# One main body for all engines, without a block and its closing barrier, and output tile 14 issued by ACT

## Chip, core and metric

The kernel runs on one NeuronCore of a Trainium2 chip. The core has a matrix engine (TensorE, PE in the profile; its weight loads are shown as PEld), a vector engine (VectorE, DVE), a scalar engine (ScalarE, ACT), GpSimd (POOL) and SyncE (SP), which issues transfers and waits. Each engine runs its own instructions in its own order, and they meet through semaphores only. The metric is the device time of one execution in microseconds, lower is better.

## What is computed

Two branches on the same input `x` (2048 positions of 512 channels, bfloat16), mixed by a gate for each position:

```python
x = A_x
g = _sigmoid((x * gate_w).sum(-1, keepdims=True))
a = _A_ref(x, A_wqkv, A_wo)
b = _B_ref(x, B_w1, B_b1, B_w2, B_b2)
return g * a + (1 - g) * b
```

Branch A is a dilated sliding attention of 32 heads with 16 channels each: every position attends to itself and to the positions 2, 4, ... 14 before it, and the result is projected by `wo`. Branch B normalizes each position, mixes along the 2048 positions by `w1` (to 1792 hidden rows), applies gelu, and mixes back by `w2`.

## The kernel before

The program is not written engine by engine. It is a list of operations, each with its engine, an estimated duration, and the names that it reads and writes; a planner (`_Sched`, lines 72 to 283) orders them. `schedule` runs a list scheduler three times: at each step it takes, over all engines, the ready operation with the earliest start, ties going to the one with the longest work behind it (`bl`). A transfer counts as an operation of its issuing engine (`dma`, 0.5 us of issue for an output write). `plan_waits` then gives every operation the semaphore waits that it needs and that its engine doesn't know to be met already. The result is one list of operations for each engine.

`emit_engine` (lines 969 to 995) writes such a list out: for each operation its waits, then its instruction, then the increment of its semaphore. Behind SP's list it puts waits for all output writes, one semaphore for each of `ds_out[0]` to `ds_out[3]` and one for `ds_outb`:

```python
            if eng_name == OUTQ:
                for d in ds_out + [ds_outb]:
                    n_ = len([o for o in sch.ops if o.is_dma and o.dsem is d])
                    if n_:
                        e.wait_ge(d.handle, 16 * n_)
```

Line 336 opens a block, `nc.Block()`. Lines 997 to 1015 call `emit_engine` inside five functions, `block.sync` to `block.tensor`, so that each engine's instructions form a body of that engine; on leaving the block, all engines meet in a barrier: each drains its pipeline, GpSimd collects their arrivals and releases them. The profile puts these closing instructions at L335, the line of the `with` that holds the block, and the opening instructions (constants written by GpSimd, and a barrier that the program always begins with) at L1029.

The work goes in this order. Loads, the first of them transposing, bring `x` and the weights in (L430, L461 and L468 are the helpers that issue transfers). TensorE projects q, k and v (L594), with some warming matmuls before (L526), and VectorE forms the products of q and shifted k (L665), which TensorE sums over the heads' channels (L673). Then TensorE does the two large mixes of branch B, L787 with `w1` and L837 with `w2`, while VectorE does the softmax and the weighted sum of v, and ACT issues 32 copies (L430) that spread the attention weights. ACT adds the bias and scales branch B by 1 - g (L904).

The last stage is the projection by `wo`. `emit_wo` (lines 863 to 883) is called for the 16 output tiles of 128 positions each. For tiles 0 to 11 a tile is one piece of 512 columns, for tiles 12 to 15 two halves, a and b, of 256 columns: four matmuls (L853) and one eviction on VectorE (L874), which multiplies by g and adds branch B's value. Behind the evictions the tile is written to the output, tiles 0 to 14 by one transfer of 128 KB on SP's queue, with the semaphore `ds_out[i % 4]`, tile 15 by two of 64 KB: its first half on SP, its second on ACT with `ds_outb`.

Of the kernel before, what the change touches and what calls it, by code (L numbers as in the profile page):

```python
# [13 lines left out]
D = 512  # L14
# [4 lines left out]
NST = S // 128  # L19
# [269 lines left out]
def _views(nc, es):  # L289
    off = {}  # L290
    cur = [0]

    def region(name, nbytes):
        nbytes = (nbytes + 63) // 64 * 64
        off[name] = cur[0]
        cur[0] += nbytes

    region("X", NST * D * 2)
    region("XT", 4 * S * 2)
    region("WQKV", 4 * 3 * D * 2)  # L300
    region("W1W", 4 * NST * 256 * 2)
    region("PBUF", 2 * 4 * S * 2)
    region("WO", 4 * D * 2)
    region("Q5", 4 * S * 2)
    region("K5", 4 * KROW * 2)
    region("V5", 4 * KROW * 2)
    region("ATX", 8 * NW * HC * 2)
    region("ATT", NW * SC * 2)
    region("OUTS", 4 * D * 2)
    region("BR", 128)  # L310
    region("BT", 128)
    region("IDENT", 128 * 2)
    region("RP", 32 * 2)
    region("SMALL", 2048)
    total = cur[0]
    arena = es.enter_context(nc.sbuf_tensor("arena", [128, total], U8))

    def view(name, dtype, dims, extra=0):
        base = arena[:].bitcast(dtype)
        pstride = base.ap[0][0]  # L320
        esz = mybir.dt.size(dtype)
        assert off[name] % esz == 0
        return bass.AP(base.tensor, off[name] // esz + extra, [[pstride, 128]] + [list(d) for d in dims])

    def pview(name, dtype, p0, np_, dims, extra=0):
        base = arena[:].bitcast(dtype)
        pstride = base.ap[0][0]
        esz = mybir.dt.size(dtype)
        return bass.AP(base.tensor, p0 * pstride + off[name] // esz + extra, [[pstride, np_]] + [list(d) for d in dims])

    return view, pview, off, total


def bass_gated_mix__sliding_local_dilated__mixer_token_mlp__prompt_kernel(nc, A_x, A_wqkv, A_wo, B_x, B_w1, B_b1, B_w2, B_b2, gate_w, out, dbg=None):
    with contextlib.ExitStack() as es:  # L335
        block = es.enter_context(nc.Block())
        view, pview, off, total = _views(nc, es)
        ps = es.enter_context(nc.psum_tensor("ps", [128, 8, 512], FP32))
        esem = {e: es.enter_context(nc.semaphore("sem_" + e)) for e in ("pool", "act", "dve", "pe")}
        sch = _Sched()  # L340
# [6 lines left out]
        outv = out[0].rearrange("(t p) d -> p t d", p=128)  # L347
# [21 lines left out]
        T1 = view("X", BF16, [(D, NST), (1, D)])  # L369
# [33 lines left out]
        def col(v_, i):  # L403
            return bass.AP(v_.tensor, v_.offset + i, [list(v_.ap[0]), [1, 1]])
# [24 lines left out]
        def mk_dma(dst, src):  # L429
            return lambda e: e.dma_start(dst, src)  # L430
# [115 lines left out]
        for hf in range(2):  # L546
            t0 = 8 * hf
            for t in range(t0, t0 + 8):
                A("dve", (lambda t_: (lambda e: e.bn_stats(out=ST6[:, t_, :], in_=X[:, t_, :])))(t), 0.59,  # L549
                  reads=["x%d" % t], writes=["st6_%d" % t], name="ln1_%d" % t, prio=0)  # L550
# [13 lines left out]
              reads=["zc%d" % hf], writes=["sd%d" % hf], name="ln_sqrt%d" % hf, prio=0)  # L564
            A("dve", (lambda t0_: (lambda e: e.reciprocal(out=cols(RSTD, t0_, 8), in_=cols(SD, t0_, 8))))(t0), 0.25,
              reads=["sd%d" % hf], writes=["rstd%d" % hf], name="ln_rstd%d" % hf, prio=0)
# [43 lines left out]
        for (b0, d0, d1) in ((0, 0, 1), (0, 1, 2), (0, 2, 3), (0, 3, 4), (4, 0, 2), (4, 2, 4)):  # L610
            s0, s1 = 0, 512
            for b in range(b0, b0 + 4):
                tn, dl = first[b]
                last_main[0] = A("pe", f_proj(tn, dl, 0, b, d0, d1, s0, s1), 0.216 * (d1 - d0) * (s1 - s0) / 512,
                                 reads=["xt0h%d" % (d0 // 2)] + ["wqkv%d_%d" % (tn, dt) for dt in range(d0, d1)],
# [11 lines left out]
        for (tn, dl, sb) in seq_proj:  # L627
# [3 lines left out]
                             reads=xr + ["wqkv%d_%d" % (tn, dt) for dt in range(4)],  # L631
# [15 lines left out]
        for t in range(NST):  # L647
# [7 lines left out]
          reads=["th"], writes=["g"], name="g_g", prio=0)  # L655
        A("dve", lambda e: e.tensor_scalar(out=OMG, in0=TH, scalar1=-0.5, scalar2=0.5, op0=ALU.mult, op1=ALU.add), 0.15,
          reads=["th"], writes=["omg"], name="g_omg", prio=0)
        A("dve", lambda e: e.tensor_tensor(out=C2, in0=OMG, in1=B2C, op=ALU.mult), 0.15,
          reads=["omg", "b2c"], writes=["c2"], name="g_c2", prio=0)
# [25 lines left out]
        for wh in range(2):  # L685
# [6 lines left out]
            for (dl, c0, nc_) in pieces:  # L692
# [3 lines left out]
                  reads=["q5_%d_%d" % (dl, sb) for sb in range(c0, c0 + nc_)] +  # L696
# [3 lines left out]
            for wl in range(4):  # L700
                qop = A("pe", f_qkr(list(enumerate(bufs)), (wl,)), 0.92, reads=rd, writes=["lg%d_0" % (4 + wl), "lg%d_1" % (4 + wl)],
                        name="qkr_%d_%d" % (wh, wl), prio=-100 + wl, delay=BURST_DELAY)
                A("act", (lambda wh_, wl_: (lambda e: e.activation(out=ATT[:, :, 4 * wh_ + wl_, :], in_=ps[:, 4 + wl_, :].rearrange("p (h c) -> p h c", h=2), func=AF.Copy)))(wh, wl),  # L703
                  0.55, reads=["lg%d_0" % (4 + wl), "lg%d_1" % (4 + wl)], writes=["lw%d" % (4 * wh + wl)],
                  name="lev_%d_%d" % (wh, wl), prio=0)
# [24 lines left out]
        for hf in range(2):  # L730
# [3 lines left out]
              reads=["outs1"], writes=["lh%d" % hf] + (wall if hf == 0 else []), name="sm_sub%d" % hf, prio=0)  # L734
            if hf == 0:
                A("act", lambda e: e.activation(out=col(SD, 0), in_=col(ZC, 0), func=AF.Exp, scale=0.0), 1.5,
                  reads=["zc0"], writes=["sd0"], name="sm_pre")
            A("act", (lambda hf_, l_: (lambda e: e.activation(out=ATT[:, hf_], in_=l_, func=AF.Exp)))(hf, lgh), 1.95,  # L738
              reads=["lh%d" % hf], writes=["att%d" % hf], name="sm_exp%d" % hf, prio=0)
        for hf in range(2):  # L740
# [5 lines left out]
            def f_rcp(e, hf_=hf):  # L746
# [6 lines left out]
              reads=["rs%d" % hf], writes=["att%d" % hf], name="sm_nrm%d" % hf, prio=0)  # L753
# [4 lines left out]
        for u in range(8):  # L758
            c, hf = u // 2, u % 2
            ds_at = sch.dsem("atx%d" % u)  # L760
            for a_ in range(4):
                dst = bass.AP(ATX.tensor, ATX.offset + a_ * pst + u * NW * HC, [[4 * pst, 32], [1, NW * HC]])
                sch.dma("act", mk_dma(dst, psub(ATT, 32 * c, 32, hf * NW * HC, [(1, NW * HC)])), 32 * NW * HC * 2, ds_at, issue=0.62,
                        reads=["att%d" % hf], writes=["atx_%d_%d" % (u, a_)], deps=pb_readers, name="d_atx_%d_%d" % (u, a_))
        USEQ = [0, 2, 1, 3, 4, 6, 5, 7]
        for k_, u in enumerate(USEQ):
# [6 lines left out]
              reads=v_res + ["atx_%d_%d" % (u, a_) for a_ in range(4)], writes=[pn] + [qk_res, k_all][k_ % 2], name="avm_%d" % u)  # L773
# [30 lines left out]
        for ft in range(NFT):  # L804
# [5 lines left out]
              reads=["acc%d" % bank, "b1c"], writes=["ut%d" % ft] + ALLXT + ["xt0h0", "xt0h1"],  # L810
              name="gel_%d" % ft, prio=0)
# [30 lines left out]
        def WB(i):  # L842
            return (4 + i) % 8

        def WBN(i):
            b_ = WB(i)
            return ["acc%d" % b_] if b_ < 4 else ["lg%d_0" % b_, "lg%d_1" % b_]
# [10 lines left out]
        ds_out = [sch.dsem("out%d" % k) for k in range(4)]  # L858
        ds_outb = sch.dsem("outb")
# [3 lines left out]
        def emit_wo(i):  # L863
            parts = [(0, D)] if i < HT0 else [(0, D // 2), (D // 2, D)]
            ons = []
            for h, (c0, c1) in enumerate(parts):
                k_ = i if len(parts) == 1 else HT0 + 2 * (i - HT0) + h
                bank, bn = WB(k_), WBN(k_)
                sfx = "" if len(parts) == 1 else "ab"[h]
                frac = (c1 - c0) / D  # L870
                on = "o%d%s" % (i, sfx)
                ons.append(on)
                A("pe", f_wo(i, bank, c0, c1), 0.866 * frac, reads=["ot%d" % (i // 2), "wo"], writes=bn, name="wo_%d%s" % (i, sfx), prio=0)
                A("dve", (lambda i_, b_, c0_, c1_: (lambda e: e.scalar_tensor_tensor(  # L874
                    out=T1[:, i_, c0_:c1_], in0=ps[:, b_, 0:c1_ - c0_], scalar=col(G, i_), in1=T1[:, i_, c0_:c1_],
                    op0=ALU.mult, op1=ALU.add)))(i, bank, c0, c1), 0.08 + 0.67 * frac, reads=bn + ["g", "t1_%d" % i], writes=[on],
                  name="cmb_%d%s" % (i, sfx), prio=0)
                if i == NST - 1:
                    q = "act" if sfx == "b" else "sp"
                    sch.dma(q, mk_dma(outv[:, i, c0:c1], T1[:, i, c0:c1]), 128 * (c1 - c0) * 2,  # L880
                            ds_out[i % 4] if q == "sp" else ds_outb, issue=0.5, reads=[on], name="d_out%d%s" % (i, sfx))
            if i < NST - 1:
                sch.dma("sp", mk_dma(outv[:, i, :], T1[:, i, :]), 128 * D * 2, ds_out[i % 4], issue=0.5, reads=ons, name="d_out%d" % i)

        p3bank = {}

# [8 lines left out]
        for i in range(NST):  # L895
# [4 lines left out]
            elif i > 1:  # L900
# [5 lines left out]
              reads=["acc%d" % bank, "omg", "c2"], writes=["t1_%d" % i, "x%d" % i],  # L906
              name="t1_%d" % i, prio=0)
# [61 lines left out]
        def emit_engine(eng_name, e):  # L969
            for op in sch.order[eng_name]:  # L970
                for d in op.waits:
                    if d.is_dma:
                        e.wait_ge(d.dsem.handle, 16 * d.seq)
                    else:
                        e.wait_ge(esem[d.eng], d.seq)
                r = op.fn(e)
                if dbg is not None:
                    rr = r[-1] if isinstance(r, list) else r
                    dbg.setdefault("opmap", []).append((eng_name, op.name, rr.ins.name, op.start, op.end))
                if op.is_dma:  # L980
                    r.then_inc(op.dsem.handle, 16)
                elif op.sig:
                    if isinstance(r, list):
                        r = r[-1]
                    r.then_inc(esem[eng_name], 1)
            if eng_name == "sp" and dbg is not None and "keep" in dbg:
                for d in sch.dsems:
                    n_ = len([o for o in sch.ops if o.is_dma and o.dsem is d])
                    if n_ and d.queue == "sp":
# [4 lines that stand above are left out]
                    if n_:  # L994
                        e.wait_ge(d.handle, 16 * n_)

        @block.sync
        def _(e):
            emit_engine("sp", e)

        @block.gpsimd
        def _(e):
            emit_engine("pool", e)

        @block.scalar
        def _(e):
            emit_engine("act", e)

        @block.vector
        def _(e):  # L1010
            emit_engine("dve", e)

        @block.tensor
        def _(e):
            emit_engine("pe", e)


# [26 lines left out]
```

## Time and profile before

| | us |
|---|---|
| median of three runs | 169.53 |
| lowest and highest | 168.92, 169.91 |
| the profiled execution | 169.25 |
| its span, first to last instruction | 167.5 |
| outside the span (169.25 - 167.5) | 1.75 |
| TensorE matmuls busy | 163.4 |
| VectorE busy | 150.8 |
| ScalarE busy | 74.7 |
| granted TensorE clock, mean | 1.000 |

The span is what the rows of the profile cover; what lies outside it is not resolved by any row. In the rows, a `q` behind an engine's name means its sequencer: waits, branches, drains and issues of transfers, which don't count as busy time. `EVENT_SEMAPHORE` is a wait or a semaphore update of its own, `DRAIN` waits until the engine's pipeline is empty. In a timeline row come start, length (both us), engine, line, operation, written and read tensor, and the count of instructions merged into the row. In the row of a line come shortest, median and longest duration in ns, and the starts of the first and the last in us.

### The profile page before, as it was taken

The numbers are of one execution on the slowest core, as the hardware profiler recorded it, in microseconds if no ns is written. First come the engines' busy times: TensorE is split into PE (matmuls) and PEld (weight loads), VectorE is DVE, ScalarE is ACT, GpSimd is POOL, SyncE is SP. The second block draws the span as 40 slices with busy tenths as digits, with TensorE's granted clock in tenths as the row PEclk, the third lists the DMA queues.
The fourth block names the chain that finished last, engine by engine and source line by source line (L and its number), as shares of the span: only waits on it lengthen the run. The fifth ranks groups of instructions, "written<-read, shape, count | busy, mean of one in ns | idle before, by whom it ended". The sixth has DMA issues, their size and how long they took to land.

```text
span 167.5 us, 2155 instructions
## 1 busy us (share of the span) xinstructions
PE 163.4 (98%) x857; PEld 77.5 (46%) x857; DVE 150.8 (90%) x155; ACT 74.7 (45%) x115; POOL 0.8 (0%) x8
## 2 busy tenths in 40 slices
PE   8899999999999999999999999999999999999993
PEld 2355555544554444444444444444444444444462
DVE  0019999999999998799999999999999999999995
ACT  3087788888899827881221221231321312210000
POOL 1000000000000000000000000000000000000000
PEclk9999999999999999999999999999999999999999
DMA  5999999979204849996799806373574380000554
GB/s 129 256 253 225 239 342 301 291 230 294 83 0 122 287 137 250 297 257 162 167 295 330 270 10 157 92 210 84 145 219 126 94 223 0 0 0 0 185 181 139
DMA packets 47625, 29.64 MB, mean 177 GB/s; under 512 B 9856, under 2 KB 46464, under 8 KB 47616
## 3 DMA queue, kind: packets, MB, share of 16 engines
q1 hardware_dynamic: 45664, 24.98, 55.6%
q10 hardware_dynamic: 1952, 4.52, 9.8%
q8 instruction: 7, 0.11, 0.3%
q14 instruction: 2, 0.02, 0.0%
HBM read 21.11 MB, written 2.10 MB: 139 GB/s over the span
## 4 chain that ended last, share of the span: by engine, by line
PE 93%; DMA 3%; DVE 2%; issue 0%
PE ps L787 29%; PE ps L837 29%; PE ps L594 25%; PE ps L853 6%; PE ps L673 4%; DMA arena<-in_A_x_dram 3%; DVE arena L874 2%
## 5 line engine op out<-in xcount | busy, mean ns | idle before, releaser
L787 PE MATMUL ps<-arena 128*128 128x512 bf16 x224 | 48.7, 379 | 0.0
L837 PE MATMUL ps<-arena 128*128 128x512 bf16 x224 | 48.7, 379 | 0.0
L665 DVE TENSOR_TENSOR arena<-arena 128x4096 bf16<-128x4096 bf16 (+2 forms) x14 | 35.7, 2590 | 10.2 <-ACT arena L605 10.2
L594 PE MATMUL ps<-arena 128*128 128x512 bf16 x192 | 41.8, 380 | 0.7 <-DMA arena<-in_A_x_dram 0.7
L772 DVE TENSOR_TENSOR arena<-arena 128x8192 bf16<-128x8192 bf16 x8 | 35.0, 4418 | 0.0
L787 PEld LDWEIGHTS ps<-arena 128*128 128x128 bf16 x224 | 21.8, 98 | 26.6 <-issue 0.4
L837 PEld LDWEIGHTS ps<-arena 128*128 128x128 bf16 x224 | 21.9, 98 | 26.5
L594 PEld LDWEIGHTS ps<-arena 128*128 128x128 bf16 x192 | 21.6, 113 | 21.1 <-issue 1.8
L904 ACT ACTIVATE arena<-ps,arena 128x512 bf16<-128x512 f32 x16 | 12.4, 778 | 39.4 <-PE ps L837 39.4
L775 DVE TENSOR_TENSOR arena<-arena 128x4096 bf16<-128x4096 bf16 (+1 forms) x16 | 27.0, 1751 | 0.0
L605 ACT ACTIVATE arena<-ps 128x512 bf16<-128x512 f32 x32 | 18.6, 596 | 4.7 <-PE ps L594 4.7
L808 ACT ACTIVATE arena<-ps,arena 128x512 bf16<-128x512 f32 x14 | 9.6, 687 | 22.9 <-PE ps L787 17.3
L853 PE MATMUL ps<-arena 128*128 128x512 bf16 (+1 forms) x80 | 14.2, 337 | 0.0
L602 ACT ACTIVATE arena<-ps 128x512 bf16<-128x512 f32 x16 | 9.0, 596 | 7.5 <-PE ps L594 7.4
L573 ACT ACTIVATE arena<-arena 128x512 bf16<-128x512 bf16 x16 | 12.2, 808 | 0.0
L874 DVE SCALAR_TENSOR_TENSOR arena<-ps,arena 128x512 bf16<-128x512 f32 (+1 forms) x20 | 11.5, 638 | 0.6 <-PE ps L853 0.4
L853 PEld LDWEIGHTS ps<-arena 128*128 128x128 bf16 x80 | 7.8, 98 | 6.2
L649 DVE SCALAR_TENSOR_TENSOR arena<-arena 128x512 bf16<-128x512 bf16 x16 | 10.0, 684 | 0.0
L549 DVE BATCH_NORM_STATS2 arena<-arena 128x6 f32<-128x512 bf16 x16 | 9.9, 680 | 0.0
L719 DVE TENSOR_TENSOR arena<-arena 128x512 bf16<-128x512 bf16 (+4 forms) x11 | 7.3, 667 | 1.2 <-ACT arena L738 0.8
L673 PE MATMUL ps<-arena 128*32 128x512 bf16 x128 | 7.3, 380 | 0.0
L703 ACT ACTIVATE arena<-ps 128x512 bf16<-128x512 f32 x8 | 4.7, 592 | 3.7 <-PE ps L673 3.7
(38 smaller groups left out, 39.2 us busy)
## 6 DMA issues: line engine op xcount, KB each, us to landing
arena<-in_B_w_dram SPq DMA_DIRECT2D x7, 1024.0 KB, 8.2
arena<-in_B_w_dram SPq DMA_DIRECT2D x8, 896.0 KB, 5.2
arena<-arena ACTq DMA_DIRECT2D x32, 128.0 KB, 2.7
arena<-in_A_x_dram SPq DMA_DIRECT2D x4, 512.0 KB, 5.8
out_dram<-arena SPq DMA_DIRECT2D x15, 128.0 KB, 1.7
arena<-in_A_x_dram SPq DMA_DIRECT2D x1, 1536.0 KB, 7.9
arena<-in_A_wqkv_dram SPq DMA_DIRECT2D x2, 256.0 KB, 3.8
arena<-in_A_x_dram SPq DMA_DIRECT2D x2, 256.0 KB, 3.2
```

The costliest lines, as they stand in the source:

```text
L573: A("act", (lambda t_: (lambda e: e.activation(out=X[:, t_, :], in_=X[:, t_, :], func=AF.Identity, scale=col(RSTD, t_), bias=col(NMR, t_)) ...
L594: ins = e.matmul(ps[:, bank, s0:s1], lhsT=lhsT, rhs=XT[:, dt, sb * 512 + s0:sb * 512 + s1], start=(dt == 0 and s0 == 0), stop=(dt == 3))
L605: return lambda e: e.activation(out=dst, in_=ps[:, bank, :], func=AF.Copy)
L665: return lambda e: e.tensor_tensor(out=PBL[buf][:, :, 512 * c0:512 * (c0 + nc_)], in0=in0, in1=in1, op=ALU.mult)
L673: ins = e.matmul(ps[32 * c:32 * c + 32, 4 + wl, :], lhsT=RP, rhs=PBL[buf][:, wl, c * 512:(c + 1) * 512], start=(dl == 0), stop=(dl == 3), ...
L772: A("dve", (lambda o_, i0, i1: (lambda e: e.tensor_tensor(out=o_, in0=i0, in1=i1, op=ALU.mult)))(pv, in0, in1), 4.4, reads=v_res + ["atx_% ...
L775: A("dve", (lambda pv_, n__: (lambda e: e.tensor_tensor(out=pv_[:, 0:n__], in0=pv_[:, 0:n__], in1=pv_[:, n__:2 * n__], op=ALU.add)))(pv, n ...
L787: ins = e.matmul(ps[:, bank, :], lhsT=W1W[:, slot, st, 128 * e_:128 * e_ + 128], rhs=X[:, st, :], start=(st == 0), stop=(st == NST - 1))
L837: ins = e.matmul(ps[:, bank, :], lhsT=W2S[slot][:, ft, 128 * e_:128 * e_ + 128], rhs=UT[:, ft, :], start=(ft == 0), stop=(ft == NFT - 1))
L853: ins = e.matmul(ps[:, bank, 0:c1 - c0], lhsT=OT[:, t, 128 * i:128 * i + 128], rhs=WO[:, t, c0:c1], start=(t == 0), stop=(t == 3))
L874: A("dve", (lambda i_, b_, c0_, c1_: (lambda e: e.scalar_tensor_tensor(out=T1[:, i_, c0_:c1_], in0=ps[:, b_, 0:c1_ - c0_], scalar=col(G, i ...
L904: A("act", (lambda i_, bank_: (lambda e: e.activation(out=T1[:, i_, :], in_=ps[:, bank_, :], func=AF.Identity, scale=col(OMG, i_), bias=co ...
```

## The change

The block is not opened any more. The five engines' lists are written one after the other straight into the program's main body, by a loop over the engines; there are no bodies to branch into, no branch out of them, and no barrier behind them. The opening barrier at the program's beginning is not touched, and neither are SP's final waits for the output semaphores. Tile 14's output write is given to ACT's queue in place of SP's, and its semaphore is `ds_outb` in place of `ds_out[2]`; SP's final waits count accordingly.

```diff
-        block = es.enter_context(nc.Block())
         view, pview, off, total = _views(nc, es)
...
             if i < NST - 1:
-                sch.dma("sp", mk_dma(outv[:, i, :], T1[:, i, :]), 128 * D * 2, ds_out[i % 4], issue=0.5, reads=ons, name="d_out%d" % i)
+                q = "act" if i == NST - 2 else "sp"
+                sch.dma(q, mk_dma(outv[:, i, :], T1[:, i, :]), 128 * D * 2, ds_out[i % 4] if q == "sp" else ds_outb, issue=0.5, reads=ons, name="d_out%d" % i)
...
-        @block.sync
-        def _(e):
-            emit_engine("sp", e)
-
-        @block.gpsimd
-        def _(e):
-            emit_engine("pool", e)
-
-        @block.scalar
-        def _(e):
-            emit_engine("act", e)
-
-        @block.vector
-        def _(e):
-            emit_engine("dve", e)
-
-        @block.tensor
-        def _(e):
-            emit_engine("pe", e)
+        for eng_name, e in (("sp", nc.sync), ("pool", nc.gpsimd), ("act", nc.scalar), ("dve", nc.vector), ("pe", nc.tensor)):
+            emit_engine(eng_name, e)
```

## The prediction

> **What bounds the kernel now.** I read the head of the page first, then the chain of waits, and then the rows of the first and the last microsecond one by one, because the change touches only these two ends.
>
> ```profile
> span 167.5 us, 2155 instructions
> PE 163.4 (98%) x857; PEld 77.5 (46%) x857; DVE 150.8 (90%) x155; ACT 74.7 (45%) x115; POOL 0.8 (0%) x8
> q8 instruction: 7, 0.11, 0.3%
> ```
>
> ```profile
> 0.73 0.07 issue
> 0.80 4.44 DMA arena<-in_A_x_dram
> 5.25 0.14 issue
> 5.38 32.11 PE ps L594 x148
> ...
> 154.49 6.92 PE ps L853 x32
> 161.41 0.03 issue
> 161.44 3.98 DVE arena L874 x9
> ```
>
> TensorE is busy for 98% of the span, and from 5.38 to 161.41 us the chain is nothing but its matmuls. No edit touches a matmul, its operands or its waits, so some 156 us stay as they are. What can change lies before 5.38 and after 161.44. At the head the chain is the first transposing load from 0.80 to 5.25, started 0.07 us after the opening barrier let SP go. At the tail it is the last evictions of VectorE, up to 165.42, and then the following stretch, in which no compute engine works:
>
> ```profile
> 165.45:167.02 1.57, 0.00 (x0) 0.00 (x0) 0.00 (x0) 0.00 (x0) 0.00 (x0) 1.00 0.52 162
> 167.02:167.50 0.48, 0.00 (x0) 0.00 (x0) 0.00 (x0) 0.00 (x0) 0.00 (x0) 1.00 0.00 0
> ```
>
> The columns are the stretch, its length, busy time of PE, PEld, DVE, ACT and POOL with instruction counts, clock, DMA share and GB/s. The first stretch is the last output write in flight. In the second nothing moves at all: the granted clock is 1.00, the DMA engines stand still, and 0.48 us go by between the last landing and the end of the span. That is where the closing barrier is:
>
> ```profile
> L335 POOLq EVENT_SEMAPHORE  x2: 17/17/17, 167.3 to 167.4; - x2
> L335 POOLq DRAIN  x1: 557/557/557, 0.9 to 0.9; - x1
> L335 PEldq DRAIN  x1: 2155/2155/2155, 162.8 to 162.8; - x1
> L335 DVEq DRAIN  x1: 524/524/524, 164.9 to 164.9; - x1
> L335 ACTq DRAIN  x1: 152/152/152, 165.9 to 165.9; - x1
> L335 SPq COMPARE_BRANCH  x1: 33/33/33, 167.1 to 167.1; - x1
> L335 SPq DRAIN  x1: 7/7/7, 167.3 to 167.3; - x1
> L335 SPq EVENT_SEMAPHORE  x1: 17/17/17, 167.4 to 167.4; - x1
> ...
> L335 PEldq EVENT_SEMAPHORE  x1: 51/51/51, 167.4 to 167.4; - x1
> ```
>
> and SP's waits just before it:
>
> ```profile
> L995 SPq EVENT_SEMAPHORE  x2: 28/28/28, 166.6 to 167.0; - x2
> ```
>
> The columns are line, engine, operation, count, shortest/median/longest in ns, and first and last start in us. The reader is to see the order: SP's last wait on an output (L995) at 167.0, the branch out of its body at 167.1, its drain at 167.3, POOL collecting and releasing at 167.3 and 167.4, all engines let go at 167.4. Four of the five drains began long before the last landing, and only SP's is late. So the closing barrier costs what SP does after its last wait, and nothing else.
>
> **The change part by part.** The closing barrier goes. SP then ends with its waits on the output semaphores. There are five of them; in the old kernel two instructions at L995 and the branch share them, so the branch's share becomes one more wait of about 28 ns (L995's duration) in place of the branch's 33 ns, in the same place. What falls away is the time from the branch's end to the span's end: 167.5 - (167.1 + 0.03) = 0.37 us. The starts are printed to 0.1 us, so 0.27 to 0.47; the stretch of 0.48 us after the last landing is the ceiling, since SP must still see that landing. I take 0.37.
>
> The drains of the other engines fall away too. They cost nothing now: POOL's 557 ns begin at 0.9 us, PE's 2155 ns and DVE's 524 ns end at 165.0 and 165.4, ACT's 152 ns at 166.1, all under the last write, which is in flight until 167.02. Were a drain made up for behind the span, the dearest one that such an idle engine would need is POOL's 0.56 us.
>
> The opening. No branch into the bodies shows in the trace, so it is bounded: the engine that matters is SP, whose gap between the release and the first load is the 0.07 us "issue" at 0.73. A jump there can cost at most 0.07, and at least nothing, if the bodies followed the opening code directly. The opening barrier itself stays. PE's gap speaks for little: it is let go at 0.7 for 51 ns, and its first weight load starts at 0.81, in this row:
>
> ```profile
> L1029 PEldq EVENT_SEMAPHORE  x1: 51/51/51, 0.7 to 0.7; - x1
> ...
> 0.81 0.14 PEld L526 LDWEIGHTS ps<-const-bfloat16-1.0 128*128 128x128 bf16 x2 [0.81 <-issue]
> ```
>
> I take 0.03, about the middle. All of it would count, because the load at 0.80 is on the chain and TensorE is full behind it.
>
> By the Trainium skill (Runtime: NRT & Kernel Launch, Instruction fetch mechanics) a taken branch to a page that isn't at hand stalls its engine for a fetch by DMA. The q8 row gives the price of one fetch here: 0.3% of 16 engines' 167.5 us is 8.0 us over 7 packets, 1.15 us each. By that rule the opening and the closing branch would give back up to 2.3 us, 167.2 in place of 169.5. The stretch from 0.73 to 0.80 and the one from 167.1 to 167.3 are too short to hold such a fetch, so the trace speaks against the rule here, and it is only rival D.
>
> Output tile 14 on ACT. One issue of 128 KB leaves SP's queue and enters ACT's, with the semaphore of tile 15's second half. The rows are:
>
> ```profile
> 164.50 0.92 DVE L874 SCALAR_TENSOR_TENSOR arena<-ps,arena 128x256 bf16<-128x256 f32 x2
> 164.57 0.33 SPq L430 DMA_DIRECT2D out_dram<-arena  x1
> 164.93 0.48 DVE L874 SCALAR_TENSOR_TENSOR arena<-ps,arena 128x256 bf16<-128x256 f32 x1
> 165.01 0.37 SPq L430 DMA_DIRECT2D out_dram<-arena  x1
> 165.45 0.36 ACTq L430 DMA_DIRECT2D out_dram<-arena  x1
> ```
>
> ```profile
> L430 SPq DMA_DIRECT2D out_dram<-arena x16: 332/333/813, 154.2 to 165.0; - x16
> L430 ACTq DMA_DIRECT2D arena<-arena x32: 477/616/1194, 74.9 to 104.5; - x32
> DMA to landing us min/median/max: 1.6/1.7/2.4
> ```
>
> The evictions are those of tile 15's two halves (the first row merges both, the third is the second alone). SP's two issues are tile 14 and the first half of tile 15, ACT's is the second half. The lower fence has the issue times of all output writes and of ACT's copies, and the time to landing of all output writes. SP is through with tile 14 at 164.57 + 0.33 = 164.90. The eviction that tile 15's first half waits for ends at 164.50 + 0.48 = 164.98, and the issue follows at 165.01. So SP holds nothing up, and taking tile 14 from it brings nothing: gain 0. In ACT's queue tile 14 would be issued at about 164.57 too. With the 0.36 us of ACT's own output issue ACT is free at 164.93, with the median of its 128 KB copies, 0.62, at 165.19, and it is needed again when the last eviction ends at 164.93 + 0.48 = 165.41. Both are early enough: loss 0. The one issue as long as 1.19 would end at 165.76 and make tile 15's second half about 0.35 late; this end I keep for the range. Behind tile 14's issue in ACT's queue stands only that second half, and the final wait of SP waits for it. The two writes also share 16 DMA engines as before; tile 14's data is 0.88 us of issue ahead of the second half's, so its landing should stay at 1.6.
>
> In the planner (an estimate per engine of 0.5 us for either queue) nothing depends on an output write, so no other order should move.
>
> **The sum.** Against the profiled execution, 169.25 us with 1.75 us outside its span: 0.37 at the end, 0.03 at the opening, 0 for tile 14 make 0.40, so 168.85, and a span of 167.1. The median of the three runs shown is 169.53, 0.28 above the profiled one, and carried over to it the forecast is 169.13. I give 169.1.
>
> **The rivals.**
>
> A, the time outside the span shrinks too. The 1.75 us outside it are not resolved. If what follows the program is again a meeting of the engines, four of them now reach it early (POOL after 1.5 us of the span, the others by 165.8), where they came at once with SP before. The nearest row for what that could hide is the longest drain of an idle engine, 0.56; with 0.40 that makes 0.96 less, 168.57, which is just beyond half a percent. For it: the engines do part early. Against: SP is still last, and it had the shortest drain, 7 ns, so most of such a meeting is behind SP's arrival either way. The Trainium skill (the same page, The ~15µs preamble/postamble breakdown) names a closing barrier of all engines of about 1.5 us; no row here shows it.
>
> B, nothing is gained. The recorded end moves, but what ends the run's time outside the span does not see it (169.53), or the drains that were hidden are done behind it: 0.40 less and 0.56 more, 169.69. For it: POOL's drain of 557 ns is free today only because it begins at 0.9 us. Against: an engine that is done early would also drain early.
>
> C, slower, by ACT's queue at the tail. [...] It begins to count when ACT's issue takes over 0.84 us (165.41 - 164.57), and the kernel is slower than before when the late start and the slow landing together exceed 0.40. For it: the slow landing did happen to an output a few microseconds earlier. Against: ACT's second half was issued at once today, behind SP's two, and nothing adds bytes.
>
> D, instruction fetches. If both branches made their engine wait for a page, at 1.15 us each as the seven fetches of the q8 row took, the time would fall by 2.3 to 167.2. Against it stand the two stretches of 0.07 and about 0.2 us into which the branches have to fit today.
>
> **How the numbers follow.** Forecast 0.53, A 0.20, B 0.13, C 0.12, D 0.02. The range: the forecast's own, with the spread of the three runs (168.92 to 169.91), is 168.6 to 169.6; A pulls the lower end to 168.2 (168.57 less the same spread), C and B the upper end to 170.0, which leaves out half of C. Half a percent, 0.85 us here, is about what a measurement of this kernel can tell from no change. Faster by more than that needs under 168.68: A, D and a little of the forecast's low end, 0.25. Slower by more, over 170.38, is the upper half of C (0.06), the upper end of B with the spread on top (0.03) and a poor draw of the rest (0.02), 0.11. Within: 0.64.
>
> **What would show it.** Right: no closing rows at all; SP's waits as the last instructions, at about 167.0 to 167.1; span 167.1; 15 output issues on SP and two on ACT, the first at about 164.6 and the second still at 165.4 to 165.5; time outside the span still 1.75. The opening term is right if the gap before the first load falls below 0.07. The forecast is wrong if the time outside the span moves by more than 0.3 either way (A or B), if the last issue of ACT is later than 0.05 after the last eviction (C), or if TensorE's chain, 5.38 to 161.41, changes its length.

## The result, and the profile after

| | before | after |
|---|---|---|
| median of eight runs, us | 169.43 | 168.38 |
| lowest and highest, us | 168.92, 169.91 | 167.84, 168.72 |
| the profiled execution, us | 169.25 | 168.05 |
| its span, us | 167.5 | 166.8 |
| outside the span, us | 1.75 | 1.25 |

The ratio of after to before is 0.9937, with a 95% interval of 0.9917 to 0.9958: 1.07 us of 169.43 are gone, between 0.7 and 1.4. That is more than twice the 0.40 that was forecast as likeliest, lies inside the stated range (168.2 to 170.0), and is close to rival A (0.96).

The head of the page after:

```profile
span 166.8 us, 2144 instructions
PE 163.2 (98%) x857; PEld 77.6 (47%) x857; DVE 150.8 (90%) x155; ACT 74.7 (45%) x115; POOL 0.8 (0%) x8
q8 instruction: 7, 0.11, 0.3%
```

The same engine work, and 11 instructions fewer in the records: the twelve of the closing rows at L335 are gone, and SP has one more wait. The q8 row has seven packets as before, so no instruction fetch fell away with the branches. The chain of waits, as start, length and what:

```profile
0.73 0.07 issue
0.80 4.18 DMA arena<-in_A_x_dram
4.98 0.14 issue
5.11 32.11 PE ps L593 x148
...
154.23 6.92 PE ps L852 x32
161.15 0.03 issue
161.17 3.98 DVE arena L873 x9
```

TensorE's pieces have the same lengths as before (32.11, ... 6.92), and so has VectorE's at the end (3.98). The gap before the first load is 0.07 as before. The first load took 4.18 us in place of 4.44, and so everything behind it stands 0.27 earlier; that is the load's own variation rather than the change, for it is issued at the same 0.80, and its length doesn't follow the block: in a kernel below that keeps the block it took 4.26, in two others without one 4.20 and 4.96:

```profile
0.80 4.26 DMA arena<-in_A_x_dram
0.80 4.20 DMA arena<-in_A_x_dram
0.80 4.96 DMA arena<-in_A_x_dram
```

(in this order: tile 14 alone on ACT, the barrier at the end, the final waits on ACT).

Then the tail, in the table by stretches (from the last issue of ACT to the last landing, and from there to the end):

```profile
165.18:166.74 1.56, 0.00 (x0) 0.00 (x0) 0.00 (x0) 0.00 (x0) 0.00 (x0) 1.00 0.64 196
166.74:166.80 0.06, 0.00 (x0) 0.00 (x0) 0.00 (x0) 0.00 (x0) 0.00 (x0) 1.00 0.00 0
```

and the rows of SP's final waits and of the output writes:

```profile
L995 SPq EVENT_SEMAPHORE  x3: 17/28/28, 165.1 to 166.8; - x3
```

```profile
L429 SPq DMA_DIRECT2D out_dram<-arena x15: 332/332/1177, 153.9 to 164.7; - x15
L429 ACTq DMA_DIRECT2D out_dram<-arena x2: 338/346/353, 164.3 to 165.2; - x2
...
DMA to landing us min/median/max: 1.6/1.7/2.8
```

The last write is in flight for 1.56 us, against 1.57 before. Behind it 0.06 us are left where 0.48 were: 0.42 gained. So the 1.20 us between the two profiled executions are 0.27 of the first load, which is chance, 0.42 of the closing rows, and 0.50 outside the span (1.75 less 1.25), with 0.01 in flight. The largest of these parts is the one outside the span, which is in no row at all. The experiments are mostly about it.

What is the same in all of them: the time outside the span is a run's time less its span (spans are given to 0.1 us), averaged over all runs of a kernel. What lies ahead of the first row can't be told apart in it from what lies behind the last; but most kernels below differ from the changed one in their ends alone, so the differences are put down to the end. It varies little (standard deviation 0.03 to 0.07), while the span itself varies from run to run with the first loads, which is why the ratios have wider intervals.

### The profile page after: what moved, and what is told of

It is laid out like the page before. It is cut to its first block, busy times and chain, and to the rows that moved or that the text cites. A ratio compares the mean times of both kernels' runs of the same rounds, so it can differ in the third digit from the quotient of the medians.

```text
span 166.8 us, 2144 instructions
## 1 busy us (share of the span) xinstructions
PE 163.2 (98%) x857; PEld 77.6 (47%) x857; DVE 150.8 (90%) x155; ACT 74.7 (45%) x115; POOL 0.8 (0%) x8
## 4 chain that ended last, share of the span: by engine, by line
PE 94%; DMA 3%; DVE 2%; issue 0%
PE ps L786 29%; PE ps L836 29%; PE ps L593 25%; PE ps L852 6%; PE ps L672 4%; DMA arena<-in_A_x_dram 3%; DVE arena L873 2%
```

## Experiments

**Which half of the change.** First kernel: the changed one with tile 14 back on SP.

```diff
-                q = "act" if i == NST - 2 else "sp"
+                q = "sp"
```

> The block is taken away as in the change; output tile 14 stays on SP's queue. If the block is the whole of it (theory 1), this is the changed kernel again: 1.0 to 1.1 us under before, time outside the span about 1.25, closing rows gone. If moving tile 14 carries part of it (rival), the time falls between the two kernels and the last write of ACT starts later after its eviction than in the changed kernel.

Measured: ratio 0.9936 (0.9891 to 0.9981); outside the span 1.28 (12 runs). It is the changed kernel again (0.9937 and 1.27), so theory 1 holds, and tile 14 is worth nothing that shows. The ratio's interval alone would hide some tenths of a us. One detail is worth a look, in the timeline of this kernel's tail:

```profile
165.15 0.92 DVE L873 SCALAR_TENSOR_TENSOR arena<-ps,arena 128x256 bf16<-128x256 f32 x2
165.31 0.95 SPq L429 DMA_DIRECT2D out_dram<-arena  x2
166.10 0.36 ACTq L429 DMA_DIRECT2D out_dram<-arena  x1
```

```profile
165.58 0.49 DVE L873 SCALAR_TENSOR_TENSOR arena<-ps,arena 128x256 bf16<-128x256 f32 x1
165.81 0.45 SPq L429 DMA_DIRECT2D out_dram<-arena  x1
```

SP issues tile 14 at 165.31 and the first half of tile 15 at 165.81, though that half was evicted at 165.15 + 0.48 = 165.63: in this execution SP was 0.18 us behind. It still cost nothing, because ACT's issue at 166.10 is the later one and its write lands last. Tile 14 on ACT would remove a lag that lies under the last write.

Second kernel: the old one, with tile 14 moved to ACT and the block kept.

> The block stays; only output tile 14 goes to ACT's queue. Theory 1: no change from before, within 0.2 us, time outside the span 1.75, closing rows as before. Rival: some tenths of a us faster, because the last landing comes earlier.

Measured: ratio 1.0013 (0.9971 to 1.0054), outside the span 1.74 (12 runs). No change, as theory 1 has it.

**Barrier, branch, or early engines.** Both kernels here start from the changed one. The first puts a barrier of all engines behind the last instruction:

```diff
             emit_engine(eng_name, e)
+        nc.all_engine_barrier()
```

> The changed kernel with a barrier of all engines behind the last instruction, in the main body, with no branch. Theory 1a (the engines that are through early do the work behind the program early): the barrier brings both parts back, span +0.2 to +0.35, outside the span 1.75, so the time is within 0.2 of before. Theory 1b (the branches and the separate closing body cost what lies outside the span): span +0.2 to +0.35, but outside the span still 1.25, so 0.7 to 0.8 under before.

Measured: ratio 1.0000 (0.9968 to 1.0031), outside the span 1.76 (12 runs). Nothing of the gain is left that the ratio can show, though there is no branch, and the time outside the span is back. The tail by stretches, for this kernel:

```profile
165.47:167.02 1.55, 0.00 (x0) 0.00 (x0) 0.00 (x0) 0.00 (x0) 0.00 (x0) 1.00 0.57 175
167.02:167.32 0.30, 0.00 (x0) 0.00 (x0) 0.00 (x0) 0.00 (x0) 0.00 (x0) 1.00 0.00 0
```

and for the second kernel, the one with the block and with tile 14 on ACT:

```profile
165.53:167.08 1.55, 0.00 (x0) 0.00 (x0) 0.00 (x0) 0.00 (x0) 0.00 (x0) 1.00 0.54 169
167.08:167.55 0.47, 0.00 (x0) 0.00 (x0) 0.00 (x0) 0.00 (x0) 0.00 (x0) 1.00 0.00 0
```

Behind the last landing the block leaves 0.47 us, a barrier without the block's branch 0.30, and no barrier 0.06. So within the span the barrier is worth 0.24 and the branch 0.17, from one profile of each kernel. SP's rows bear the branch's part out: its last wait on an output starts at 167.0 in this kernel as in the old one, and its drain at 167.1 here, at 167.3 there:

```profile
L995 SPq EVENT_SEMAPHORE  x3: 17/28/28, 165.4 to 167.0; - x3
L999 SPq DRAIN  x1: 7/7/7, 167.1 to 167.1; - x1
```

The other kernel has neither barrier nor drain nor branch, but all five engines wait for the output writes:

```diff
-            if eng_name == OUTQ:
+            if True:
                 for d in ds_out + [ds_outb]:
```

> The changed kernel, in which every engine, not SP alone, waits for all output writes at its end; no barrier, no drain, no branch. All five are through at the same moment. Theory 1a (early engines): span as the changed kernel's within 0.1, outside the span back at about 1.75. Theory 1b (branches and closing body): outside the span 1.25, the time the changed kernel's.

```profile
L995 POOLq EVENT_SEMAPHORE  x3: 17/43/43, 165.9 to 167.7; - x3
L995 DVEq EVENT_SEMAPHORE  x3: 21/50/50, 165.9 to 167.7; - x3
L995 PEldq EVENT_SEMAPHORE  x3: 51/51/51, 165.9 to 167.7; - x3
L995 SPq EVENT_SEMAPHORE  x3: 17/28/28, 166.1 to 167.7; - x3
L995 ACTq EVENT_SEMAPHORE  x3: 17/38/38, 166.4 to 167.7; - x3
```

All five are through with their last waits at 167.7. Measured: outside the span 1.82 (12 runs), ratio 0.9989 (0.9954 to 1.0025). That is theory 1a: the half microsecond outside the span depends on when the engines end, not on a barrier's instructions, a drain or a branch. Theory 1b falls. Rival D falls too: without the branches the changed kernel gained 1.07 us and not 2.3, with as many fetches as before, and here half a microsecond of it is lost again without a branch. In the span this kernel should keep most of the 0.42; the ratio's interval is too wide to show it.

**Which engine.** In four kernels the final waits are at the end of one other engine's list, so that this engine alone is late and SP is early. Nothing else differs:

```diff
-OUTQ = "sp"
+OUTQ = "act"
```

(and "pool", "dve", "pe").

> The changed kernel with the waits for all output writes at the end of ACT's list in place of SP's, so that ACT alone is late. Span as the changed kernel's within 0.1. Theory 2a (each engine has a remainder of its own behind the program, and the slowest one counts): the time outside the span is ACT's remainder, anything between 0.9 and 1.8, and among the four engines tried so at least one gives 1.8. Theory 2b (the engines meet one after another, and what counts is how many come late at once): 1.2 to 1.4 for each of the four, none gives 1.8.

> The same with the waits at the end of POOL's list. Theory 2a: POOL has the dearest drain of an idle engine (557 ns in the kernel before), so it is the likeliest to have the long remainder: 1.8 outside the span. Theory 2b: 1.2 to 1.4.

> The same with the waits at the end of VectorE's list. Theory 2a: its own remainder, between 0.9 and 1.8. Theory 2b: 1.2 to 1.4.

> The same with the waits at the end of TensorE's list. Theory 2a: its own remainder, between 0.9 and 1.8; its wait takes 51 ns where SP's takes 17 to 28, so the span is up to 0.05 longer. Theory 2b: 1.2 to 1.4.

| last engine | outside the span, us | standard deviation | runs | ratio to before |
|---|---|---|---|---|
| SP (the changed kernel) | 1.27 | 0.03 | 8 | 0.9937 (0.9917 to 0.9958) |
| VectorE | 1.37 | 0.05 | 10 | 0.9937 (0.9905 to 0.9968) |
| ACT | 1.44 | 0.05 | 10 | 0.9955 (0.9907 to 1.0002) |
| TensorE | 1.53 | 0.06 | 10 | 0.9938 (0.9896 to 0.9981) |
| POOL | 1.82 | 0.03 | 10 | 0.9981 (0.9936 to 1.0026) |
| all five (above) | 1.82 | 0.05 | 12 | 0.9989 (0.9954 to 1.0025) |

In the profile behind POOL's row of the table, its last wait ends the span of 167.4:

```profile
L995 POOLq EVENT_SEMAPHORE  x3: 17/43/43, 163.6 to 167.3; - x3
```

The ratios don't tell the first four apart, the times outside the span do. POOL alone gives what all five give together, so theory 2a holds and 2b falls: each engine has a time of its own, here called its remainder, between its last instruction and the point where the run's time ends. The figures of the table are these remainders plus the same unknown part ahead of the first row, so only their differences are the engines' own. POOL's is the longest, SP's the shortest. With any meeting of all engines at the end, POOL's counts; with SP alone at the end, SP's.

**Does the latest remainder count?** Two kernels to try that rule on numbers not yet seen. In the first POOL waits too, but only for the writes up to the first half of tile 15:

```diff
+            if eng_name == "pool":
+                e.wait_ge(ds_out[3].handle, 64)
             if eng_name == OUTQ:
```

> The changed kernel, in which POOL too waits at its end, but only for the writes up to the first half of tile 15, which lands 0.3 to 0.4 us before the last write; SP waits for all as before. Theory 2a (each engine's own remainder, the latest counts; POOL's is 1.82 and SP's 1.27): POOL's remainder ends 1.82 - 0.35 after SP's last instruction, so 1.4 to 1.5 outside the span. If POOL's long remainder only shows when it is the last engine to come (rival): 1.27.

```profile
L992 POOLq EVENT_SEMAPHORE  x1: 17/17/17, 167.5 to 167.5; - x1
```

```profile
L997 SPq EVENT_SEMAPHORE  x3: 17/28/28, 166.3 to 167.9; - x3
```

POOL's last instruction starts at 167.5, SP's at 167.9, so POOL's remainder should end 1.82 - 0.4 = 1.4 after SP's. Measured: 1.50 outside the span (10 runs, standard deviation 0.07), where the rival has 1.27. The rule holds within 0.1, and a POOL that is not last still counts. The 0.1 by which it falls short is more than the scatter of ten runs and stays unexplained. Ratio 0.9931 (0.9887 to 0.9976).

In the second all engines but POOL wait for everything:

```diff
-            if eng_name == OUTQ:
+            if eng_name != "pool":
```

> The changed kernel, in which SP, ACT, VectorE and TensorE all wait for all output writes at their ends, and POOL alone is through early. Theory 2a: the longest of the four remainders counts, TensorE's, so 1.5 to 1.6 outside the span, 0.25 to 0.3 less than with POOL among them. Rival (the number of engines that come at once counts): close to 1.8.

Measured: 1.58 (10 runs, standard deviation 0.06), TensorE's 1.53 within the scatter, and well below the 1.77 of the old kernel's runs beside it. Ratio 0.9956 (0.9915 to 0.9996). The difference to all five is 0.24, at the edge of what was expected. How many engines come at once doesn't matter within this scatter; which one does.

The rule also fits the old kernel. In its trace POOL's last row ends at 167.40, 0.09 before the end of the span, so the rule gives 1.82 - 0.09 = 1.73, more than the 1.53 of TensorE, whose row ends the span; 1.77 to 1.79 were measured.

No kernel tried is clearly better than the changed one: of the five engines on which the final waits can stand, SP has the shortest remainder.

## Why the prediction was right and wrong

**The stated range: right, but not by the forecast's mechanism.** The forecast's own part of the range doesn't hold the measured 168.38. By the spread of the three runs it is 168.5 to 169.5 (168.92 and 169.91 less 0.40; the prediction has 168.6 to 169.6), and A's lower end by the same spread is 168.0 rather than 168.2. The range holds the result only because rival A, with a chance of 0.20, was given room in it. Half of the gain came by A's way.

**That it gets faster, and by what at the closing rows: right, the size a little short.** The term was 0.37, from the branch's end to the end of the span. Measured are 0.42. The step that was off is "the branch's share becomes one more wait ... in the same place". The five waits are paired differently in the new program: the single one comes first, at 165.1, and the last of the three starts at 166.8 as the last landing comes. No wait follows it. The ceiling of 0.48 that the prediction named was the better guess.

**The opening, 0.03: wrong, it is 0.** The old program does begin each engine's list with a jump into its body, and closes it with one. SP's two jumps, which the new program doesn't have, are

```
-L997 UnconditionalBranch
...
-L335 UnconditionalBranch
```

But the gap before the first load is 0.07 in the chain of both kernels. Either the jump is not in the loaded program or it is hidden; the rows don't tell which. Of the closing jumps, too, only SP's has a row, and that one carries one of the five final waits.

**Tile 14, 0: right.** Alone it gives 1.0013 (0.9971 to 1.0054); left out of the change, the ratio stays at 0.9936. In the timeline of the changed kernel

```profile
164.31 0.35 ACTq L429 DMA_DIRECT2D out_dram<-arena  x1
...
164.66 0.48 DVE L873 SCALAR_TENSOR_TENSOR arena<-ps,arena 128x256 bf16<-128x256 f32 x1
...
165.18 0.34 ACTq L429 DMA_DIRECT2D out_dram<-arena  x1
```

ACT is through with tile 14 at 164.66, and it issues the second half of tile 15 at 165.18, 0.04 after the last eviction's end (164.66 + 0.48). Rival C did not come: the longest output issue on ACT was 353 ns here and 382 in any kernel above. So no run shows the late start of 0.35 that the prediction keeps for ACT's queue, and on which, with B, the upper end of its range, 170.0, rests. SP did have a long issue (1177 ns), but earlier. Three long issues have one thing in common in the traces: ACT's of 1194 ns and SP's of 813 in the old kernel start at 81.5 and 163.0, while a packet of the instruction queue (q8) is in flight, 81.3 to 82.3 and 162.6 to 163.5, and SP's of 1177 in the new one starts at 162.7 during such a packet, 162.3 to 163.5. Not every issue during such a packet is long (one took 332 ns in the kernel with the final waits on ACT), and how a packet would make one long is not shown.

**The time outside the span, taken as unchanged: the step that failed.** The prediction carried 1.75 us over from the old kernel as a constant. It is 1.27, and the difference is half of the gain. Rival A had the mechanism, engines that are through early do early what they have to do behind the program, and with 0.56 for the longest drain also nearly the size: 1.79 (the old kernel's 35 runs beside the first four kernels) less 1.27 is 0.52 (0.51 with the 1.28 of the kernel without a block in the same series). The argument held against it was "SP is still last, and it had the shortest drain, 7 ns, so most of such a meeting is behind SP's arrival either way". Its first half is true and the conclusion doesn't follow. What lies behind the last instruction is not one common stretch that begins when the last engine comes; it has a length for each engine, and SP, being the cheapest, is the engine by which one wants to be late. The larger price of the old barrier was that it made POOL late, and so "the closing barrier costs what SP does after its last wait, and nothing else" was true of the span alone. The prediction's own sign for this, "the time outside the span moves by more than 0.3", is what the result showed.

The Trainium skill (Runtime: NRT & Kernel Launch, The ~15µs preamble/postamble breakdown) has a closing barrier of all engines of about 1.5 us behind the kernel. All that lies outside the span is of that order here, 1.27 to 1.82 us, whatever part of it is the closing barrier, and it depends on which engine comes last. What each engine does in its remainder is not resolved here: that POOL's 0.55 us more than SP's are the same kind of work as its 557 ns drain is suggested by the size alone.

**Summed up.** 0.42 in the span, from one profile of each kernel, and 0.52 outside it are 0.94, against 1.07 (0.7 to 1.4) measured.

## What to carry to other kernels

When the last thing that a kernel does is to wait for its output, let only SP do it, and let the other engines run out of instructions: the block with its closing barrier cost 0.9 us here, half of it where no row of the profile shows it. So compare the run's time with its span for both kernels, and don't carry the difference over as a constant. A transfer moved to another queue brought nothing, even with its old queue 0.18 us behind, because another queue had the write that lands last.

## What the runs showed of the hardware

The time between an engine's last instruction and the end of the counted run differs by engine. With one engine alone late, the time outside the span is 1.27 us for SP, 1.37 VectorE, 1.44 ACT, 1.53 TensorE, 1.82 POOL, each with the same unknown part ahead of the first row. The end of the run is the latest of the engines' ends within 0.1 us, also for an engine that is 0.4 us ahead of the last (1.50 measured, 1.4 by the rule). The final wait is recorded with 28 ns on SP, 38 on ACT, 43 on POOL, 50 on VectorE and 51 on TensorE. A branch at the end of SP's list, one that carries a wait, cost 0.17 us between the last landing and the end (0.47 against 0.30 us, one profile each), of which its own row shows 33 ns.
